# Sixteen gate/up steps placed beside the exponentials of an S4 + SwiGLU forward and backward kernel, with a re-laid prologue

## The chip, the cores and the metric

The kernel runs on one core of one Trainium2 chip. The metric is device time in microseconds for one launch; the figure of a kernel is the median of its runs. A profiled execution shows, for each engine (PE = TensorE, with its weight loads apart as PEld; DVE = VectorE; ACT = ScalarE; POOL = GpSimd; SP = SyncE, which here only issues transfers), what ran when and what it waited for.

## The reference

With x of 2048 tokens by D = 576 channels, N = 128 states, F = 4608 hidden units:

```python
xn = layernorm(x)                                  # no weights, eps 1e-5
dt = exp(log_dt)[:, None]
P  = exp((dt * A)[:, :, None] * arange(L))         # D x N x L, complex
K  = einsum("dn,dnl,dn->dl", C, P, dt * B).real    # the kernel of the convolution
s  = irfft(rfft(pad(xn)) * rfft(pad(K)))[:L] + xn * Dskip
gate, up = xn @ w1, xn @ w3
g  = silu((silu(gate) * up) @ w2)
out = x + s * g
```

The kernel returns `out` and, for a given `grad_out`, the gradients of x, of the seven S4 parameter matrices and vectors (real and imaginary parts apart), of Dskip, and of w1, w3, w2.

## The kernel before, in words

One program, in stages whose instructions a scheduler interleaves by priority. `pre(us)` and `at(us)` set the priority of what follows (`pre` for the prologue, in units of 600 for one us; `at` in units of 1000, behind all of `pre`). A `Chain` keeps the operations that go through it in program order on their engine, and `issue_after(x)` puts an instruction behind x in that order. So the order on an engine is fixed before the launch; on the chip each engine runs its list in order and waits by semaphores.

Prologue (`prologue`, L264). The 2048 tokens are 16 tiles of 128 rows; the odd tiles are held in reversed order of rows (`odd_A_u`, written by one transfer and read back). `ln_stats` (L169) and `ln_normalise` (L186) give `xn_bf` (tokens on partitions), and PE transposes, eight tiles at a time, give `xnT` (channels on partitions; its last 64 channels stand twice, the second copy made by an SP transfer). The S4 kernel is not evaluated state by state over 2048 points: l is split into two digits, and exp and the phases are made for short tables. For that, rho = dt · A_re is split into three bf16 pieces (`split3`, L374), stored (`PCS_dram`) and read back as `lhs_r`; a selector row matrix SELR (built from index rows) times `lhs_r` gives exponents in PSUM (`e_ps`, 128x1024 f32, two buffers), ACT takes the exponential (`early_exps`, L498; 54 of them, the product at L514), and the table goes to `E_dram` in 18 stores of 3072 columns. `early_spectra` (L519) multiplies folded sums of `xn_bf` (held in the `xt` tiles) by DFT matrices `cCS` (product at L533, eviction by DVE at L537) and stores the spectrum of the input, `UH_dram`.

Gate and up products (`ffn_hidden`, L859). 9 blocks of 512 hidden units by 8 pairs of token tiles are 72 steps. A step multiplies 2 tiles by 512 columns of w1 and of w3: 16 products 128x128x512 (L901) and 4 tail products for the last 64 channels (L909, two at a time on the two halves of the array). pg and pu, two PSUM buffers each, take them. ACT writes silu(gate) into s_t (L913), copies up into u_t (L918), and copies the gate of the first tile into g_t (L917); DVE copies the gate of the second (L915) and multiplies h_t = s_t · u_t (L920). H goes out on SP's queue, G and U on POOL's, for the backward pass.

Interleaved with it, by due times in its argument: `ssm_forward` (L469), which is `ssm_kernel` (L542) with 36 chunks of 16 channels, and then `ssm_conv` (L788). A chunk loads its part of `E_dram` (SP), makes phases by 12 products 128x256 (`et_ps`, L589), takes sines on ACT (`cs_k`, L590, six of 512 columns), multiplies on DVE (`q_k`, `p_k`, `t_k`, `v_k`), and sums over states by 64 small products (`kps`, L626). The convolution comes in two halves of the channels; each makes the spectra of the kernel, multiplies them with `UH_dram` on DVE (complex products, `cm_t` and `V`, L777 to L786), and transforms back (L761). Its small loads (Dskip, the reversed `grad_out`, the DFT matrices turned into `cT` over `CS_dram`) are issued on SP at the opening of `ssm_forward`. PSUM has eight banks of 512 f32 columns: beside the gates, `s_ps` (three) and `s_ps1` (one).

After both come `ffn_output` (L927, the product with w2 and the output) and `backward` (L1344).

Of the kernel before, what the change touches and what calls it, by code (L numbers as in the profile page):

```python
# [10 lines left out]
ACT = mybir.ActivationFunctionType  # L11
# [6 lines left out]
P = 128  # L18
# [58 lines left out]
class K:  # L77

# [47 lines left out]
    def setup_consts(self):  # L126
# [3 lines left out]
        self.pre(2)  # L130
# [4 lines left out]
        self.eps_col = const.tile([P, 1], FP32, name="eps_col")  # L135
        nc.vector.memset(self.eps_col[:], 1e-5)
# [6 lines left out]
        self.irow = const.tile([P, 512], FP32, name="irow")  # L143

    def pre(self, us):
        self.tc.cur_priority = int(us * 600)
# [9 lines left out]
    def ln_load(self, sb):  # L156
        nc, cfg = self.nc, self.cfg
        xf = self.aps["A_u"].flatten_outer_dims()
        self.xs, self.xts = [], []
        for b in range(cfg.LT // 4):  # L160
            xt = sb.tile([P, 4, cfg.D], BF16, name=f"xt{b}")
            rows = xf[4 * b * P:4 * (b + 1) * P, :].rearrange("(i two p) d -> two p i d", two=2, p=P)
            nc.sync.dma_start(out=xt[:, 0:4:2, :], in_=rows[0])
            self.xs += [xt[:, i, :] for i in range(4)]
            self.xts.append(xt)
        for b, xt in enumerate(self.xts):
            nc.sync.dma_start(out=xt[:, 1:4:2, :], in_=self.odd["A_u"][2 * b:2 * b + 2].rearrange("i p d -> p i d"))

    def ln_stats(self, sb, small):  # L169
        nc, cfg = self.nc, self.cfg  # L170
        D, LT = cfg.D, cfg.LT
        half = D // 2
        self.mv = sb.tile([P, LT, 2], FP32, name="mv")
        for i in range(LT):
            stats = small.tile([P, 2, 6], FP32, name="stats")
            self.V.bn_stats(stats[:, 0, :], self.xs[i][:, 0:half])
            self.V.bn_stats(stats[:, 1, :], self.xs[i][:, half:D])
            if i > 0:
                self.V.bn_aggr(self.mv[:, i - 1, :], last[:])
            last = stats  # L180
        self.V.bn_aggr(self.mv[:, LT - 1, :], last[:])
# [4 lines left out]
    def ln_normalise(self, sb, ps):  # L186
        nc, cfg = self.nc, self.cfg
        D, LT, DT = cfg.D, cfg.LT, cfg.DT
        nfull = D // P
        rem = D - nfull * P  # L190
        negmr = sb.tile([P, LT], FP32, name="negmr")
        self.V.scalar_tensor_tensor(out=negmr[:], in0=self.mv[:, :, 0], scalar=-1.0, in1=self.rstd[:], op0=ALU.mult,
                                       op1=ALU.mult)
        TB = 8
        for tb in range(0, LT, TB):
            for i in range(tb, tb + TB):
                self.V.tensor_scalar(out=self.xn_bf[:, i, :], in0=self.xs[i], scalar1=self.rstd[:, i:i + 1],
                                        scalar2=negmr[:, i:i + 1], op0=ALU.mult, op1=ALU.add)
            if tb > 0:
                self.dft_rows()  # L200
            tsl = slice(tb * P, (tb + TB) * P)
            for c, (do, dsz) in enumerate(cfg.dch):
                pt = ps.tile([P, TB * P], BF16, name="ln_pt")
                for j in range(TB):
                    nc.tensor.transpose(pt[:dsz, j * P:(j + 1) * P], self.xn_bf[:, tb + j, do:do + dsz],
                                        self.ident_bf[:])
                self.V.tensor_copy(out=self.xnT[:dsz, c, tsl], in_=pt[:dsz, :])
            nc.sync.dma_start(out=self.xnT[rem:P, nfull, tsl], in_=self.xnT[0:rem, nfull, tsl])
        for b in range(LT // 4):
# [54 lines left out]
    def prologue(self, matp, selp, xp):  # L264
# [6 lines left out]
        self.rstd = self.persist.tile([P, LT], FP32, name="rstd")  # L271
        self.xnT = xp.tile([P, DT, L], BF16, name="xnT")
        self.PCS_dram = self.dram.tile([3, 3, D, N], BF16, name="PCS_dram")
        mul = lambda e, o, a, b: e.tensor_tensor(out=o[:], in0=a[:], in1=b, op=ALU.mult)
        with pool(name="par_tmp", bufs=1) as tmp, pool(name="sel_tmp", bufs=1) as st, pool(name="ln_sb", bufs=1) as lsb, \
                pool(name="ln_small", bufs=4) as small, pool(name="dftgen", bufs=1) as dg, \
# [1529 lines left out]
```

## Time and profile before

| | us |
|---|---|
| median of 3 runs (lowest to highest) | 1875.47 (1872.55 to 1878.48) |
| the profiled execution, own time | 1874.95 |
| its span | 1873.2 |
| PE busy, share of the span | 1689.1, 90% |
| DVE busy | 1370.1, 73% |
| ACT busy | 910.0, 49% |
| POOL busy | 352.1, 19% |
| first product of the exponentials | starts at 35.59 |
| last exponential | starts at 126.15 |
| first gate product | 126.98 |
| first sine of a kernel chunk (cs_k) | 152.26 |
| last v_k of the chunks | starts at 428.11 |
| first product of the output stage | 601.45 |

How to read it: the whole-span shares average over stages with different limits, so the table gives the edges of the stages too; they come from the timeline (start, duration, engine, line, operation, output <- inputs, and in brackets the idle time before and what ended it). A group's row in the view by line has, behind the count, the busy time, the mean of one in ns, and the idle time of its engine just before it with what ended it. The view by stretch gives, for each, the engines' busy time, the granted clock of PE, the busy share of the 16 DMA engines, and GB/s.

### The profile page before, as it was taken

How to read it: one execution, taken by the hardware profiler on the slowest of the kernel's cores; microseconds unless marked ns; L12 is line 12 of the kernel's file. 1: busy time of each engine (PE TensorE's matmuls, PEld its weight loads, DVE VectorE, ACT ScalarE, POOL GpSimd, SP SyncE). 2: the span in 40 equal slices, each digit the busy share in tenths (PEclk: the TensorE clock that was granted, in tenths of full speed). 3: DMA queues.
4: the chain of work that ended last, by engine and by line, in shares of the span. 5: the costliest groups of instructions: out<-in, count | busy, mean ns of one | idle time of the engine just before them, and what ended most of it. 6: DMA issues, size and time to landing. Idle time of an engine off the chain costs nothing. (4 is left out here: it accounts for less than half of the span.)

```text
span 1873.2 us, 38325 instructions
## 1 busy us (share of the span) xinstructions
PE 1689.1 (90%) x15461; PEld 1231.2 (66%) x15516; DVE 1370.1 (73%) x2081; ACT 910.0 (49%) x1632; POOL 352.1 (19%) x567
## 2 busy tenths in 40 slices
PE   2999999999897999799999999999998968979997
PEld 0335555555353777578878887888777756868786
DVE  5538666768988555588694989759998954867675
ACT  3768888887563111465765756565444300001001
POOL 4021222222223111011111111111110242031032
PEclk9999999999998999899999999999999998989999
DMA  6579988887777997658666575579999899988993
GB/s 172 175 242 328 328 304 305 308 291 267 239 242 225 218 205 179 218 157 232 183 198 190 180 211 173 167 210 284 258 233 232 179 221 245 209 195 204 220 210 72
DMA packets 627231, 417.27 MB, mean 223 GB/s; under 512 B 424429, under 2 KB 567853, under 8 KB 622445
## 3 DMA queue, kind: packets, MB, share of 16 engines
q1 hardware_dynamic: 569820, 281.98, 58.3%
q0 software_dynamic: 30672, 106.50, 16.8%
q10 hardware_dynamic: 26560, 26.35, 4.7%
q8 instruction: 121, 1.98, 0.4%
q14 instruction: 58, 0.47, 0.1%
HBM read 135.74 MB, written 190.89 MB: 174 GB/s over the span
## 5 line engine op out<-in xcount | busy, mean ns | idle before, releaser
L1657 PEld LDWEIGHTS <-acts 128*128 128x128 bf16 x2304 | 228.4, 100 | 100.7 <-DMA acts<-GG_dram 19.8
L1610 PEld LDWEIGHTS <-xn_bf 128*128 128x128 bf16 x2304 | 225.6, 98 | 37.0 <-issue 10.1
L1229 DVE TENSOR_TENSOR pr_q<-et_ps,pz 128x1024 f32<-128x1024 f32 x144 | 176.0, 1222 | 48.9 <-PE et_ps L1224 41.8
L1657 PE MATMUL px<-wT,acts 128*128 128x288 bf16 x1408 | 182.5, 289 | 17.3 <-DMA wT<-in_B_w_dram 17.3
L901 PEld LDWEIGHTS <-xnT 128*128 128x128 bf16 x1152 | 107.4, 98 | 115.5 <-issue 25.3
L1232 DVE TENSOR_REDUCE S_all<-pr_q 128x32 f32<-128x1024 f32 x144 | 175.3, 1217 | 3.4
L1552 PE MATMUL ph<-w2T,goT 128*128 128x256 bf16 x1440 | 173.0, 275 | 1.6 <-ACT gh L1555 1.4
L901 PE MATMUL pg<-wmB_w,xnT 128*128 128x512 bf16 x526 | 147.9, 382 | 16.4 <-DVE g_t L915 9.5
L901 PE MATMUL pu<-wmB_w,xnT 128*128 128x512 bf16 x571 | 155.4, 379 | 0.4
L1590 PE MATMUL pgw<-go_o,h_n 128*128 128x288 bf16 x1152 | 150.4, 287 | 4.1 <-DVE h_n L1530 2.8
L1552 PEld LDWEIGHTS <-goT 128*128 128x128 bf16 x1440 | 140.4, 99 | 19.7 <-issue 2.8
L1610 PE MATMUL pgw<-gu_n,xn_bf 128*128 128x256 bf16 x1152 | 135.6, 276 | 7.0 <-ACT gw L1594 6.8
L1657 PE MATMUL px<-wA,acts 128*128 128x288 bf16 x896 | 123.4, 298 | 19.6 <-DMA acts<-GG_dram 19.1
L1590 PEld LDWEIGHTS <-h_n 128*128 128x128 bf16 x1152 | 112.6, 98 | 32.5 <-DVE h_n L1530 3.3
L1610 PE MATMUL pgw<-gg_n,xn_bf 128*128 128x256 bf16 x1152 | 130.2, 273 | 1.6 <-ACT gw L1612 1.6
L913 ACT ACTIVATE s_t<-pg 128x512 bf16<-128x512 f32 x144 | 87.8, 610 | 89.4 <-PE pu L909 44.7
L1685 ACT ACTIVATE go<-gx 128x576 bf16<-128x576 f32 x16 | 10.9, 683 | 220.7 <-DVE gx L1668 220.7
L1555 ACT CAST gh<-ph 128x512 bf16<-128x512 f32 x144 | 82.0, 600 | 71.6 <-PE ph L1552 54.0
L590 ACT ACTIVATE cs_k<-et_ps 128x512 bf16<-128x512 int16 x216 | 112.1, 643 | 1.7 <-PE et_ps L589 1.3
L1612 ACT CAST gw<-pgw 128x256 bf16<-128x256 f32 x144 | 53.9, 375 | 99.3 <-PE pgw L1610 96.7
L924 POOL DMA_DIRECT2D G_dram<-g_t x72 | 52.3, 727 | 232.3 <-DVE g_t L915 223.9
L918 ACT CAST u_t<-pu 128x512 bf16<-128x512 f32 x144 | 86.9, 604 | 12.0 <-PE pu L901 12.0
(302 smaller groups left out, 3232.2 us busy)
## 6 DMA issues: line engine op xcount, KB each, us to landing
U_dram<-u_t POOLq DMA_DIRECT2D x72, 256.0 KB, 4.3
G_dram<-g_t POOLq DMA_DIRECT2D x72, 256.0 KB, 4.0
H_dram<-h_t SPq DMA_DIRECT2D x72, 256.0 KB, 4.7
Q_dram<-q_k SPq DMA_DIRECT2D x36, 512.0 KB, 4.2
h_n<-U_dram POOLq DMA_DIRECT2D x18, 1024.0 KB, 8.7
gg_n<-G_dram POOLq DMA_DIRECT2D x18, 1024.0 KB, 5.9
GU_dram<-gu_n SPq DMA_DIRECT2D x36, 512.0 KB, 3.6
GG_dram<-gg_n SPq DMA_DIRECT2D x36, 512.0 KB, 8.3
```

The source lines that it names most:

```text
L590: nc.scalar.activation(out=CS[:, :, o:o + 256], in_=pt[:].bitcast(I16)[:, :, 0::2], func=ACT.Sin, scale=6.283184 / 2 ** 16)
L901: ins = nc.tensor.matmul(pt[:], lhsT=xnT[:, c, ts], rhs=wm[w][:, c, :], start=(q == 0 and c == 0), stop=(q == 1 and c == nfull - 1))
L913: nc.scalar.activation(out=s_t[:, :, q, :], in_=pgv, func=ACT.Silu)
L918: nc.scalar.copy(out=u_t[:, :, q, :], in_=pu[:].rearrange("p (g f) -> p g f", g=ng))
L1229: nc.vector.tensor_tensor(out=pr[:].rearrange("p r k e -> p r (k e)"), in0=T[h][:].rearrange("p k z d a -> p (k z d a)")[:, None].to_broad ...
L1232: nc.vector.tensor_reduce(out=self.S_all[:, :, d0:d0 + 4], in_=pr[:].rearrange("p r k (d a) -> p (r k) d a", d=4), op=ALU.add, axis=AX.X)
L1552: self.pe_last = nc.tensor.matmul(ph[j][:, k, :].rearrange("p (a f) -> p a f", f=P), lhsT=lw, rhs=rh, start=(n == 0), stop=(n == nfull))
L1555: self.sc(lambda: nc.scalar.copy(out=gh[:, j], in_=ph[j][:]))
L1590: self.pe_last = nc.tensor.matmul(pgw[pi_][:, 0:pw], lhsT=hn[:, tt, fl * P:(fl + 1) * P], rhs=go_o[:, tt, po:po + pw], start=(tt == 0), st ...
L1610: self.pe_last = nc.tensor.matmul(pw_[:, 0:FG], lhsT=self.xn_bf[:, tt, c * P:(c + 1) * P], rhs=nat[:, tt, :], start=(tt == 0), stop=(tt == ...
L1612: self.sc(lambda: nc.scalar.copy(out=gw[:, c], in_=pw_[:, 0:FG]))
L1657: self.pe_last = nc.tensor.matmul(px[pi_][:, 0:pw], lhsT=act[:, ai, fi, :], rhs=w[:, po:po + pw], start=(n == 0), stop=(n == len(steps) - 1))
```

## The change

- The first 16 of the 72 gate/up steps (two blocks) are placed in the prologue, each tied by `issue_after` to one of the exponentials. ACT uses Tanh there in place of Silu, since it stands beside Exp: silu(g) = g · (0.5 tanh(g/2) + 0.5). POOL multiplies g · u, DVE does the rest. g_t is copied by ACT in the first four of these steps, by DVE in the others. G is stored on SP's queue, U on POOL's. In the first block a step takes two tiles of the same parity, and G and U are stored in two transfers each.
- PSUM: the gates' four banks are open in the prologue; `e_ps` has one buffer (two banks) instead of two, and one pool `t_ps` of two banks serves the transposes and the spectra, whose evictions are cut into 64 of 288 columns.
- Layer norm: even tiles first, then odd; 1/sqrt by an integer shift and three Newton steps on DVE instead of a square root on ACT; transposes four tiles at a time; the second copy of the last 64 channels is made by PE; the folded sums are made by POOL.
- Index rows are made in bf16 by POOL, in place of i32 rows and ACT casts; log_dt is loaded as rows and turned by PE. The queues: even x tiles, ten parameter loads, six stores of pieces and three `lhs_r` loads on SP; log_dt and A_re on ACT's; odd tiles and the first weights on POOL's.
- Each exponential is stored by itself (54 stores instead of 18). The convolution's small loads stand on SP behind chunk 8's load of its table.
- The other 56 steps follow a plan by hand: 38 beside the 36 chunks, 18 beside the convolution, each tied to a chunk's or a transform's last product. In the chunk stage ACT copies the gate of the first tile in two steps of three, DVE the others; in the convolution ACT copies all.

```diff
+    EARLY = 16
...
-        self.tc.cur_priority = int(us * 600)
+        self.tc.cur_priority = int(us * 1000)
...
-        sd = sb.tile([P, LT], FP32, name="sd")
-        self.S.activation(out=sd[:], in_=self.mv[:, :, 1], func=ACT.Sqrt, bias=self.eps_col[:], scale=1.0)
-        self.V.reciprocal(out=self.rstd[:], in_=sd[:])
...
+        V.tensor_scalar(out=a[:].bitcast(I32), in0=v[:].bitcast(I32), scalar1=1, scalar2=None, op0=ALU.logical_shift_right)
+        V.tensor_scalar(out=y.bitcast(I32), in0=a[:].bitcast(I32), scalar1=-1.0, scalar2=float(0x5f3759df), op0=ALU.mult,
+                        op1=ALU.add)
+        for _ in range(3):
+            V.scalar_tensor_tensor(out=a[:], in0=y, scalar=-0.5, in1=y, op0=ALU.mult, op1=ALU.mult)
+            V.tensor_tensor(out=a[:], in0=a[:], in1=v[:], op=ALU.mult)
+            V.scalar_tensor_tensor(out=y, in0=a[:], scalar=1.5, in1=y, op0=ALU.add, op1=ALU.mult)
...
+        for t0 in range(0, len(tiles), 4):
+            four = tiles[t0:t0 + 4]
+            xT = self.xnT.rearrange("p c (t q) -> p c t q", q=P)[:, :, four[0]:four[-1] + 1:2]
+            lead = self.exps[leads[t0 // 4]]
...
+                    for j, i in enumerate(four):
+                        with self.tc.issue_after(lead.ins) if c + j == 0 else nullcontext():
+                            nc.tensor.transpose(pv[:, j * P:(j + 1) * P], self.xn_bf[:, i, c * P:(c + 1) * P], self.ident_bf[:])
+                else:
+                    pv = pt[:]
...
-                self.V.tensor_tensor(out=self.xts[b][:, 2 * k:2 * k + 2, :], in0=lo, in1=hi, op=op)
+                self.G.tensor_tensor(out=self.xts[b][:, 2 * k:2 * k + 2, :], in0=lo, in1=hi, op=op)
...
-                pool(name="ex_l", bufs=1) as lp, pool(name="ex_e", bufs=3) as ep, pool(name="ex_u", bufs=2) as up, \
-                pool(name="ex_ps", bufs=2, space=PS) as eps, ExitStack() as early:
-            lps = early.enter_context(pool(name="ln_ps", bufs=2, space=PS, side="right"))
...
+                pool(name="ex_ps", bufs=1, space=PS) as eps, pool(name="t_ps", bufs=2, space=PS) as tps:
...
+            pd = tps.tile([P, 512], FP32, name="t_ps")
+            nc.tensor.transpose(pd[:].bitcast(BF16)[:, 0:DT], lr[:], self.ident_bf[0:DT, 0:DT])
+            self.S.activation(out=self.dt_col[:], in_=pd[:].bitcast(BF16)[:, 0:DT], func=ACT.Exp)
...
-            self.dma_engines, self._dma_i = [nc.sync, self.S], 0
+            self.dma_engines, self._dma_i = [nc.sync], 0
             self.split3(tmp, rho, 2)
-            self.S.copy(out=self.irow[:], in_=irow[:])
-            self.dft_angles()
-            for k, eng in enumerate((nc.sync, self.S, nc.sync)):
-                ld = eng.dma_start(out=LR_[k * 16:(k + 1) * 16],
-                                   in_=self.PCS_dram[2, k].rearrange("(k p) n -> p k n", p=16))
+            for k in range(3):
+                nc.sync.dma_start(out=LR_[k * 16:(k + 1) * 16], in_=self.PCS_dram[2, k].rearrange("(k p) n -> p k n", p=16))
+            self.dft_phases()
+            self.build_reader(SELR)
+            self.pre(6)
+            self.load_rates(tmp)
+            self.A_im = self.load_dmat(tmp, aps["A_A_im"], "A_im", fill=0.0)
             self.pre(8)
-            self.build_reader(SELR, st)
-            self.pre(10)
-            self.dft_phases()
-            self.pre(12)
+            self.dft_sines()
+            self.pre(9)
+            last = self.ln_stats(even[1:], small, last)
+            self.ln_root(even, small, last)
+            self.early_exps(SELR, LR_, ep, eps, 0, 4)
+            self.pre(18)
+            self.ln_normalise(even, tps, (2, 4))
+            self.pre(24)
+            last = self.ln_stats(odd, small)
+            self.ln_root(odd, small, last)
+            self.ln_normalise(odd, tps, (7, 10))
             self.dft_signs()
-            self.build_selectors(st, selp)
-            self.dma_engines = [nc.sync]
-            with self.tc.issue_after(ld.ins):
-                self.A_im = self.load_dmat(tmp, aps["A_A_im"], "A_im", fill=0.0)
+            self.dft_rows()
+            self.pre(30)
...
+            self.early_exps(SELR, LR_, ep, eps, 4, 12)
+            self.pre(75)
...
+            self.early_exps(SELR, LR_, ep, eps, 12, 18)
+            self.pre(42)
+            self.ln_fold()
+            self.build_selectors(st, selp)
+            self.pre(60)
...
+            self.early_spectra(up, tps, 50, 1.15)
+            self.exps_last = self.S.prev
+            for n in range(self.EARLY + 1):
+                next(gate)
...
+        self.sel_dl = dl = st.tile([P, QW + 2 * PW], BF16, name="sel_dl")
+        self.sel_val = val = st.tile([P, QW + 2 * PW], BF16, name="sel_val")
...
+        sync.prev = after
...
+        sync.dma_start(out=self.odd["grad_out"][:], in_=self.turned(self.aps["grad_out"].flatten_outer_dims()))
+        self.CS_dram = self.dram.tile([2, 2, P, cfg.LS], BF16, name="CS_dram")
+        sync.dma_start(out=self.CS_dram[:].rearrange("m i p k -> p m i k"), in_=self.cCS[:])
+        self.cT = self.matp.tile([P, 2, cfg.KT, 2 * P], BF16, name="cT")
+        for m in range(2):
+            for i in range(2):
+                sync.dma_start_transpose(out=self.cT[:, m, :, i * P:(i + 1) * P], in_=self.CS_dram[m, i])
...
+            self.exps, self.e_stores = [], []
+            self.E_dram = self.dram.tile([NCH // 2, P, 2 * TW], BF16, name="E_dram")
         for c2 in range(2 * p0, 2 * p1, 2):
...
+                e = len(self.exps)
+                self.pre(17.5 + 1.2 * e if e < 7 else 26 + 4 * (e - 7) if e < 12 else 46 + 1.9 * (e - 12))
+                E = ep.tile([P, 1024], BF16, name="E_k")
...
+                self.exps.append(self.e_last)
+                self.S.activation(out=E[:], in_=pe[:], func=ACT.Exp)
+                self.e_stores.append(nc.sync.dma_start(out=self.E_dram[c2 // 2, :, o:o + 1024], in_=E[:]))
...
+                        self.pre(T + TU * (((h * NB + m) * KT + kt) * 2 + ri))
+                        pt = ps.tile([P, 512], FP32, name="t_ps")
...
+                if ch == 8:
+                    self.conv_loads(el)
...
+                ins = nc.tensor.matmul(pt[:, k], lhsT=lhs, rhs=SEL[:, k, o:o + 256], start=True, stop=True)
+            with self.tc.issue_after(self.exps_last.ins):
+                nc.scalar.activation(out=CS[:, :, o:o + 256], in_=pt[:].bitcast(I16)[:, :, 0::2], func=ACT.Sin,
+                                     scale=6.283184 / 2 ** 16)
+        self.marks.append(ins)
...
-            self.at(T0 + TC * b)
+            self.at(T0 + TC * 4.5 * b)
...
-            self.at(T0 + TC * (NB + m))
+            self.at(T0 + TC * (18, 23, 35, 52)[m])
...
+    def gate_time(self, n):
+        if n < 4:
+            return -74 + 5 * n
+        if n < self.EARLY:
+            return -54 + 6.5 * (n - 4)
+        i = n - self.EARLY
+        return 19.2 + 7 * i if i < 38 else 285 + 8.2 * (i - 38)
+
+    def gate_mark(self, n):
+        i = n - self.EARLY
+        if i < 38:
+            return 36 * i // 38 - 1
+        h, k = divmod(i - 38, 9)
+        return 36 + 8 * h + (-1 if k == 0 else (1, 3, 4, 4, 5, 5, 6, 6)[k - 1])
+
...
+            ld = Chain(self.tc, nc.sync if fb else nc.gpsimd)
+            ld.prev = self.x_last if fb == 0 else self.e_stores[10] if fb == 1 else None
...
+                    mark = self.gate_mark(step)
+                    while due is not None and (due <= T or len(self.marks) <= mark):
+                        due = next(self.ssm, None)
+                pair = [4 * (n % 4) + n // 4 + 2 * q for q in range(NT)] if fb == 0 else [NT * n, NT * n + 1]
+                early = step < self.EARLY
...
+                if early:
+                    th = self.dftgen.tile([P, ng, NT, self.FG], BF16, name="th", tag=("dft_fr", "dft_q")[step % 2])
...
+                                    lead = None
+                                    if c + q == 0 and w == "B_w1":
+                                        if early:
+                                            lead = self.exps[6 + 3 * step // 2 if step < 4 else 12 + 7 * (step - 4) // 2]
+                                        else:
+                                            lead = self.marks[mark] if mark >= 0 else None
+                                    with self.tc.issue_after(lead.ins) if lead else nullcontext():
+                                        ins = nc.tensor.matmul(pt[:], lhsT=xnT[:, c, ts], rhs=wm[w][:, c, :],
+                                                               start=(q == 0 and c == 0), stop=(q == 1 and c == nfull - 1))
...
-                    nc.scalar.activation(out=s_t[:, :, q, :], in_=pgv, func=ACT.Silu)
-                    if q % 2 == 1:
+                    if early:
+                        nc.scalar.activation(out=th[:, :, q, :], in_=pgv, func=ACT.Tanh, scale=0.5)
+                    else:
+                        with self.tc.issue_after(self.exps_last.ins):
+                            nc.scalar.activation(out=s_t[:, :, q, :], in_=pgv, func=ACT.Silu)
+                    if step < 4 or step >= self.EARLY + 38 or (not early and q == 0 and step % 3):
+                        nc.scalar.copy(out=g_t[:, :, q, :], in_=pgv)
+                    else:
                         nc.vector.tensor_copy(out=g_t[:, :, q, :], in_=pgv)
-                    else:
-                        nc.scalar.copy(out=g_t[:, :, q, :], in_=pgv)
                     nc.scalar.copy(out=u_t[:, :, q, :], in_=pu[:].rearrange("p (g f) -> p g f", g=ng))
                 self.tail = chain
-                nc.vector.tensor_tensor(out=h_t[:].rearrange("p t (g f) -> p g t f", g=ng), in0=s_t[:], in1=u_t[:],
-                                        op=ALU.mult)
-                nc.sync.dma_start(out=self.H_dram[i0:i0 + NT, :, f0:f0 + FB].rearrange("t p f -> p t f"), in_=h_t[:])
+                hv = h_t[:].rearrange("p t (g f) -> p g t f", g=ng)
+                if early:
+                    nc.gpsimd.tensor_tensor(out=s_t[:], in0=g_t[:], in1=u_t[:], op=ALU.mult)
+                    self.at(T + 7)
+                    nc.vector.tensor_scalar(out=hv, in0=th[:], scalar1=0.5, scalar2=0.5, op0=ALU.mult, op1=ALU.add)
+                    nc.vector.tensor_tensor(out=hv, in0=hv, in1=s_t[:], op=ALU.mult)
+                else:
+                    nc.vector.tensor_tensor(out=hv, in0=s_t[:], in1=u_t[:], op=ALU.mult)
+                tsl = slice(pair[0], pair[-1] + 1, pair[1] - pair[0])
+                nc.sync.dma_start(out=self.H_dram[tsl, :, f0:f0 + FB].rearrange("t p f -> p t f"), in_=h_t[:])
                 for (dst, src) in ((self.G_dram, g_t), (self.U_dram, u_t)):
-                    nc.gpsimd.dma_start(out=dst[fb * ng:(fb + 1) * ng, :, i0:i0 + NT, :].rearrange("g p t f -> p g (t f)"),
-                                        in_=src[:].rearrange("p g t f -> p g (t f)"))
+                    if early and src is g_t:
+                        self.at(T + 3)
+                    eng = nc.sync if early and src is g_t else nc.gpsimd
+                    if fb:
+                        eng.dma_start(out=dst[fb * ng:(fb + 1) * ng, :, tsl, :].rearrange("g p t f -> p g (t f)"),
+                                            in_=src[:].rearrange("p g t f -> p g (t f)"))
+                    else:
+                        for g in range(ng):
+                            eng.dma_start(out=dst[g, :, tsl, :], in_=src[:, g])
...
+            gate = k.ffn_hidden(wp, gup, fps)
+            k.prologue(matp, selp, xp, gate)
...
-                k.ffn_hidden(wp, gup, fps, 0, 12, k.ssm_forward(0, 8, 8))
+            k.ssm = k.ssm_forward(21, 7.3, 1)
+            for _ in gate:
+                pass
```

More of the change, by code (lines that the diff above doesn't have):

```diff
@@ L166, in ln_load, with ln_load_odd @@
+        self.xs = [xt[:, i, :] for xt in self.xts for i in range(4)]
+    def ln_load_odd(self):
         for b, xt in enumerate(self.xts):
[L167 to L174, printed above, removed]
+            self.x_last = self.nc.gpsimd.dma_start(out=xt[:, 1:4:2, :],
+                                                   in_=self.odd["A_u"][2 * b:2 * b + 2].rearrange("i p d -> p i d"))
@@ L175, in ln_stats @@
+    def ln_stats(self, tiles, small, last=None):
+        half = self.cfg.D // 2
+        for i in tiles:
             stats = small.tile([P, 2, 6], FP32, name="stats")
             self.V.bn_stats(stats[:, 0, :], self.xs[i][:, 0:half])
[L177 to L181, printed above, removed]
-        sd = sb.tile([P, LT], FP32, name="sd")
@@ new lines, in ln_stats, with ln_root @@
+            self.V.bn_stats(stats[:, 1, :], self.xs[i][:, half:])
+            if last is not None:
+                self.V.bn_aggr(self.mv[:, last[0], :], last[1][:])
+            last = i, stats
+        return last
+    def ln_root(self, tiles, small, last):
+        self.V.bn_aggr(self.mv[:, last[0], :], last[1][:])
+        sl = slice(tiles[0], tiles[-1] + 1, 2)
+        self.root(small, self.rstd[:, sl], self.mv[:, sl, 1], len(tiles))
+        self.V.scalar_tensor_tensor(out=self.negmr[:, sl], in0=self.mv[:, sl, 0], scalar=-1.0, in1=self.rstd[:, sl],
+                                    op0=ALU.mult, op1=ALU.mult)
```

285 lines of the change are left out of this document (129 added, 156 removed).

## The prediction

> **What bounds the kernel now.** First view: busy time of each engine by stretch of the span; the columns are stretch, length, busy us (and instructions) of PE, PEld, DVE, ACT, POOL, granted clock, DMA share, GB/s.
>
> ```profile
> 0.00:36.00 36.00, 0.41 (x2) 0.17 (x3) 24.22 (x86) 6.18 (x7) 16.94 (x26) 1.00 0.67 181
> 36.00:127.00 91.00, 85.17 (x271) 26.42 (x270) 39.33 (x73) 65.45 (x69) 12.83 (x17) 1.00 0.58 197
> 127.00:152.00 25.00, 24.64 (x136) 12.23 (x138) 17.20 (x30) 13.22 (x24) 4.38 (x6) 1.00 0.76 255
> 152.00:428.00 276.00, 266.76 (x3513) 150.09 (x3547) 197.82 (x275) 241.03 (x478) 66.80 (x92) 1.00 0.89 310
> 428.00:601.00 173.00, 153.06 (x915) 79.10 (x930) 158.72 (x217) 96.55 (x202) 41.12 (x56) 0.96 0.73 239
> 601.00:1873.00 1272.00, 1159.10 (x10633) 963.16 (x10631) 932.76 (x1404) 487.53 (x855) 210.00 (x371) 0.97 0.81 204
> ```
>
> Five stages precede 601. PE is empty for 36 us. From 36 to 127 it looks full with only 271 instructions. From 152 to 428 (kernel chunks beside gate steps) PE is the bound. From 428 to 601 (convolution beside the last gate steps) VectorE is, 158.7 of 173. Next, the timeline where the first stage opens and where it closes:
>
> ```profile
> 35.59 1.86 PE L514 MATMUL e_ps<-SELR,lhs_r 48*128 48x512 bf16 x4 [35.59 <-DVE stats L72]
> 36.63 1.94 ACT L72 ACTIVATE E_k<-e_ps 128x1024 bf16<-128x1024 f32 x2 [17.23 <-PE e_ps L514]
> ...
> 126.15 1.02 ACT L72 ACTIVATE E_k<-e_ps 128x1024 bf16<-128x1024 f32 x1 [1.50 <-PE e_ps L514]
> 126.98 0.63 PE L901 MATMUL pg<-wmB_w,xnT 128*128 128x512 bf16 x1
> ```
>
> So the 54 exponentials run from 36.6 to 127.2 and the first gate product starts behind the last of them. The first line's releaser (stats) is only the last event seen; lhs_r was issued at 23.3 to 27.4 and lands at about 35, and that is the true wait. Then the groups by line from 36 to 127, the PE groups from 104 to 126.9, and a gate product's from 152 to 428:
>
> ```profile
> L514 PE MATMUL e_ps<-SELR,lhs_r 48*128 48x512 bf16 x108 | 54.2, 613 | 39.0 <-DVE stats L72 35.6 <-ACT E_k L72 2.3 <-ACT WT L72 1.0
> L72 ACT ACTIVATE E_k<-e_ps 128x1024 bf16<-128x1024 f32 x54 | 54.1, 1025 | 40.8 <-PE e_ps L514 40.5 <-ACT E_k L72 0.2
> ```
> ```profile
> L514 PE MATMUL e_ps<-SELR,lhs_r 48*128 48x512 bf16 x30 | 15.0, 614 | 0.7 <-ACT E_k L72 0.7
> L533 PE MATMUL u_ps<-xt,cCS 128*128 128x288 bf16 x30 | 8.8, 440 | 0.0
> ```
> ```profile
> L901 PE MATMUL pu<-wmB_w,xnT 128*128 128x512 bf16 x350 | 96.5, 379 | 0.1
> ```
>
> ACT idles 40 us for the e_ps product, and that product takes 613 ns, where the gate product of the last view, of the same 512 columns, takes 379. PE is at half rate throughout this stage, though the clock column, which shows what the throttle granted, says 1.00. Last, the rows of the convolution stage:
>
> ```profile
> L783 DVE TENSOR_TENSOR cm_t<-u,kz 128x2304 bf16<-128x2304 bf16 x20 | 26.8, 1344 | 0.0
> L915 DVE CAST g_t<-pg 128x512 bf16<-128x512 f32 x24 | 16.2, 677 | 1.2 <-ACT s_t L913 1.2
> L920 DVE TENSOR_TENSOR h_t<-s_t,u_t 128x1024 bf16<-128x1024 bf16 x24 | 16.1, 671 | 0.3 <-ACT u_t L918 0.3
> ```
>
> VectorE spends 32 us there on gate steps; its own work has no idle before it.
>
> **The change part by part.** Unit prices, as pitches from start to start: a gate step on PE is 16 full products at 0.2155 us plus 0.53 for the tails, 3.98; a chunk on PE is 12 × 0.109 (et_ps) + 64 × 0.0186 (kps) + gaps, 2.7. Check: 44.7 steps and 36 chunks make 275 against the 276.5 us measured (152.3, first cs_k, to 428.8, last v_k). On VectorE a step is 1.2 us (g_t 0.6 on average, h_t 0.6).
>
> A. Start of the exponentials, 35.6 → 27 (20 to 32). log_dt comes by rows and a PE transpose, so dt_col leaves the chain near 5 instead of 11.3, and the pieces of rho are ready by about 10. Against that, the built order puts four xt loads and ten rate loads ahead of the six PCS stores, on SP alone. At 0.6 to 0.9 us an issue (the eight rate loads took 12.96 to 20.16 before) they reach SP at 12 to 15.5 (20.2 before), the lhs_r loads at about 18 (23.4), and they land 8 after their issue, as before (27.4 to 35).
>
> B. End of the prologue, first cs_k, 152.3 → 165. The two versions differ in kind here: before, four gate steps were done by 152; now sixteen are. From 27: seven exponentials at 2.2 us (the product now waits for the activation, since e_ps has one buffer: 1.0 cold product + 1.03 + hand-off) are 15. Steps 0 to 3, with five exponentials and the odd tiles' transposes, are 24. Twelve steps with 3.5 exponentials each follow. Their PE work at full rate is 3.98 + 3.5 × 0.43 + 10.7 spectra products at 0.128 = 6.9 us; ACT's is 3.5 × 1.03 + four evictions at a pitch of 0.48 = 5.5. I take 8.0, for the waits of a single e_ps: 3.5 rounds of product, hand-off and activation at 1.8 are 6.3, which PE can't always fill. 12 × 8.0 = 96, the WT turn 3: 165, so **+12.7** (bounds 140 to 195). Tanh has no row; an eviction of the same tile costs 593 to 612 ns (Silu, copies), and I take that, down to nothing if another engine is last. Its new POOL product has no row either: POOL's 128x640 products take 1.26 to 1.53 us, so 2.0 to 2.5 for 128x1024, sixteen times, and with the folds moved there POOL is under 90 us of 138, off the path. The two VectorE operations of a step (0.7 each) and u_e copies cut into 64 halves leave VectorE at about 110 of 138. The root on VectorE adds 12 tiny operations, twice, under 0.2 us each, beside exponentials; it takes away a Sqrt.
>
> C. Kernel chunks, 276.5 → 250, **−26.3**. 37 steps × 3.98 + 36 × 2.7 = 244.5; plus 2 of edges, plus 4 where the grad_out turn, the CS store and the four cT transposes now stand on SP between chunk 8's and chunk 9's E loads. q_k waits for those loads, and v_k, kps behind it. Bounds 0 and 12. ACT then has 36 × 3.4 + 37 × 2.4 = 211 of 250 and covers the g_t copies still put there.
>
> D. Convolution, 172 → 156, **−16**. VectorE's own work is 128.5 (two halves of 64.3), plus 25 × 1.2 and 13 idle: 172 now. Eighteen steps are left and their g_t go to ACT: 128.5 + 18 × 0.6 + 17 idle. Idle 12 to 20 gives 151 to 160.
>
> E. From the first output product (601.4) the built order of instructions is the same on all engines: 0, with ±3 left for its transfers (DMA is 81% busy there).
>
> Sum: 12.7 − 26.3 − 16 = −29.6 on the profiled execution's 1874.95 (span 1873.2): 1845.4. That execution lies 0.03% below the median of the three runs, 1875.47, so no correction: **1845**.
>
> **The rivals.**
>
> Full packing. If PE never waits and is at full rate, the prologue ends at 27 + 113 = 140 (16 × 3.98 of gates, 108 × 0.2155 of e_ps, 128 × 0.128 of spectra, 10 of transposes): −12.3 − 26.3 − 16 = −54.6, **1820**. For it: gate products reached 379 ns within 1.5 us of starting at 127. Against it: one e_ps buffer, and e_ps and u_ps rows that stayed cold from 104 to 126.9 while PE was busy 23.8 of 22.9 us. Chance 0.20. [...]
>
> Cold prologue, the slower side. PE stays at half rate beside exponentials, as in all of 36 to 127, because 48-row products and waits interrupt the gate products. A step is then 7.9 + 3.5 × 0.85 + 10.7 × 0.245 = 13.5 us; 12 make 162, the prologue ends near 244, +92 − 42 = +50: **1924**. It decides once a step takes over 8.0 + 29.6/12 = 10.5 us, which is about half of the time cold. For it: rate held only at 73 to 79% busy or more elsewhere, and a 3 us gap at 510 cost it (granted clock 0.76 to 0.90 after). Against it: of a step's 6.9 us, 3.98 are products of the form that warmed at once. Chance 0.14.
>
> Transfers become the bound. DMA is 0.89 busy at 310 GB/s in the chunk stage; the same bytes in 26 us less need about 320 or more (337 was seen), and eight of the early steps store G and U in rows of 512 B instead of 1024, G on SP between the E stores. Chunks then stay at 265 to 276: 1860 to 1871, **1866**, and up to 1885 if E loads wait for the last E stores. Chance 0.12.
>
> The gain in chunks is given back in the convolution: VectorE has 128.5 of its own, and if its idle time grows from 13 to 33 us, for ACT now has every g_t there, D is nothing: **1861**. Chance 0.08. That the gates would not be moved at all is excluded: the built order shows sixteen steps before the first cs_k.
>
> **How the numbers follow.** The forecast, 1830 to 1860, has 0.46. Faster by over 0.3% (about what a measurement of this kernel can tell from no change) is the forecast, full packing, the convolution case and four tenths of the transfer case: 0.79. Within 0.3% (1870 to 1881): 0.06, from transfers and a half-cold prologue. Slower: 0.15. The range goes from 1816 (full packing with idle 12 in D) to 1877 (transfers, or two fifths of the prologue cold).
>
> **What would show it.** First exponential at 27; first cs_k at 165, with e_ps products at 613 (cold) or 379 (warm) ns and the gate products the same; ACT's idle before E_k named e_ps; last v_k at 415; first output product at 572; everything behind it of equal length. It is wrong if the products from 50 to 150 stay above 600 ns, if the chunks do not reach 7 us each, or if the last stage shifts with the layout of the early stores.

## The result, and the profile after

The changed kernel took 1967.88 us in the median of four runs (1961.28 to 1985.62), the kernel before 1876.97 beside it. The ratio is 1.0503, 95% interval 1.0429 to 1.0577. The forecast, 1845 us and a range up to 1877, had the wrong sign.

The view by stretch of the changed kernel, cut at its first cs_k, last v_k, first output product and first ph product (the first product of the backward part):

```profile
0.00:229.30 229.30, 153.12 (x682) 54.60 (x695) 138.65 (x286) 110.99 (x149) 111.90 (x102) 0.90 0.59 191
229.30:492.30 263.00, 244.62 (x3365) 140.64 (x3401) 195.18 (x279) 219.42 (x434) 55.89 (x77) 0.96 0.88 299
492.30:668.30 176.00, 132.16 (x799) 70.31 (x809) 141.38 (x188) 87.41 (x190) 38.15 (x52) 0.88 0.71 207
668.30:844.60 176.30, 157.09 (x1260) 120.68 (x1260) 90.13 (x143) 25.32 (x54) 23.98 (x46) 0.97 0.77 189
844.60:1961.90 1117.30, 1005.01 (x9372) 845.60 (x9370) 841.08 (x1258) 461.26 (x800) 179.17 (x317) 0.96 0.81 201
```

The reader is to see that PE has less work from 229 on, as planned, and that no stretch is full any more: in the prologue PE is busy 153 of 229 us and POOL 112, where POOL had 34 before. The same five lengths for all kernels (us; profiled executions):

| kernel | prologue | chunks | convolution | output | backward | span |
|---|---|---|---|---|---|---|
| before | 152.3 | 276.5 | 172.7 | 167.0 | 1104.7 | 1873.2 |
| after | 229.3 | 263.0 | 176.0 | 176.3 | 1117.3 | 1961.9 |
| e1 folds on DVE | 212.8 | 260.6 | 175.3 | 175.9 | 1114.9 | 1939.5 |
| e2 POOL cleared | 189.4 | 260.5 | 171.9 | 176.3 | 1131.9 | 1930.0 |
| e3 four early | 202.6 | 292.9 | 163.7 | 174.0 | 1119.4 | 1952.6 |
| e4 loads early | 229.3 | 248.3 | 174.1 | 175.6 | 1115.4 | 1942.7 |
| e5 halves | 244.3 | 262.4 | 174.8 | 177.7 | 1121.5 | 1980.7 |
| e6 halves, POOL cleared | 196.9 | 262.4 | 175.1 | 178.0 | 1121.5 | 1933.9 |
| e7 e6, loads early, S on POOL | 198.3 | 248.5 | 172.7 | 182.5 | 1126.7 | 1928.7 |
| e8 before again | 152.7 | 276.6 | 172.8 | 167.5 | 1104.6 | 1874.2 |
| e9 before, one e_ps | 173.5 | 283.2 | 172.0 | 171.1 | 1119.6 | 1919.4 |
| e10 two e_ps, POOL cleared, loads early | 187.2 | 248.4 | 175.9 | 176.4 | 1115.2 | 1903.1 |
| e11 e10, H load held | 184.0 | 247.3 | 165.4 | 176.7 | 1117.7 | 1891.1 |
| e12 before, 54 stores | 150.8 | 278.6 | 172.1 | 168.5 | 1114.1 | 1884.1 |
| e13 e11, H loads in order | 185.3 | 247.3 | 164.5 | 167.6 | 1131.0 | 1895.7 |
| e14 e13 with four early | 161.6 | 276.2 | 162.1 | 190.9 | 1115.7 | 1906.5 |

Against before, the change is +77.0, −13.5, +3.3, +9.3 and +12.6: 88.7 us of span. The lengths come from one profiled execution each; e7, e13 and e14 have four timed runs, the other experiments the profiled one alone. The kernel before, timed beside them, took 1902.32 us (e1 to e4, one run), 1881.30 (e5 to e8), 1876.33 (e9 to e12, one run) and 1881.38 (e13, e14), so the lengths of stages are compared, not the totals.

### The profile page after: what moved, and what is told of

Its sections match the earlier page's. It is cut to its first block, busy times and chain, and to the rows that moved or that the text cites. A ratio compares the mean times of both kernels' runs of the same rounds, so it can differ in the third digit from the quotient of the medians.

```text
span 1961.9 us, 38537 instructions
## 1 busy us (share of the span) xinstructions
PE 1692.0 (86%) x15472; PEld 1231.8 (63%) x15533; DVE 1406.4 (72%) x2153; ACT 904.4 (46%) x1625; POOL 409.1 (21%) x594
## 5 line engine op out<-in xcount | busy, mean ns | idle before, releaser
L1328 DVE TENSOR_TENSOR pr_q<-et_ps,pz 128x1024 f32<-128x1024 f32 x144 | 176.0, 1222 | 53.7 <-PE et_ps L1323 46.2
L982 PE MATMUL pg<-wmB_w,xnT 128*128 128x512 bf16 x524 | 155.2, 402 | 23.3 <-ACT g_t L1000 16.3
L1020 POOL DMA_DIRECT2D G_dram<-g_t x56 | 40.6, 725 | 289.3 <-DVE g_t L1002 163.9
L1694 POOL DMA_DIRECT2D out_dram<-gw x36 | 20.0, 555 | 372.0 <-ACT gw L1693 319.1
```

What stands on the lines that cost most here:

```text
L982: ins = nc.tensor.matmul(pt[:], lhsT=xnT[:, c, ts], rhs=wm[w][:, c, :], start=(q == 0 and c == 0), stop=(q == 1 and c == nfull - 1))
L1020: eng.dma_start(out=dst[fb * ng:(fb + 1) * ng, :, tsl, :].rearrange("g p t f -> p g (t f)"), in_=src[:].rearrange("p g t f -> p g (t f)"))
L1328: nc.vector.tensor_tensor(out=pr[:].rearrange("p r k e -> p r (k e)"), in0=T[h][:].rearrange("p k z d a -> p (k z d a)")[:, None].to_broad ...
```

## The experiments

**Theory 1**, formed on the trace of after: operations of POOL stop VectorE's, and PE stands behind them. Its lines in the timeline of the changed kernel (start, duration):

```profile
60.89 2.11 POOL L1007 TENSOR_TENSOR s_t<-g_t,u_t 128x1024 bf16<-128x1024 bf16 x1 [1.08 <-ACT u_t L1003]
...
61.06 1.97 DVE L72 SCALAR_TENSOR_TENSOR rt_a<-rstd 128x8 f32<-128x8 f32 x1
...
64.03 13.09 DVE L72 TENSOR_SCALAR xn_bf<-xt,rstd,negmr 128x576 bf16<-128x576 bf16 x8
...
64.97 11.99 POOL L72 TENSOR_TENSOR xt<-xn_bf 128x1152 bf16<-128x1152 bf16 x5 [0.55 <-DVE xn_bf L72]
```

```profile
86.87 7.00 POOL L72 TENSOR_TENSOR xt<-xn_bf 128x1152 bf16<-128x1152 bf16 x3
...
88.06 0.14 DVE L72 TENSOR_SCALAR rp<-pcol 128x1 f32<-128x1 f32 x1
...
88.30 5.59 DVE L72 TENSOR_TENSOR rp<-rp,rc 128x1 f32<-128x1 f32 x1
...
94.11 0.16 DVE L72 TENSOR_TENSOR rs<-rs,rc 128x1 f32<-128x1 f32 x1
```

A root step of eight columns, usually 0.17 us, lasts 1.97 and ends with the POOL product at 63.0. A product of one column with two inputs lasts 5.59 us and ends with the last of three folds at 93.9, without getting in between them; the same form takes 0.16 when POOL is idle. An operation with a single input, at 88.06 beside the same folds, takes its 0.14. So this is no sharing of bandwidth: the operation waits until the other engine's has ended. The xn_bf operations, with one tensor as input, show the same: 13.09 us for eight of them, five of which last 2.46 us each, one beside each of five folds, where the others last 0.42; before, all eight took 2.81:

```profile
54.69 2.81 DVE L72 TENSOR_SCALAR xn_bf<-xt,rstd,negmr 128x576 bf16<-128x576 bf16 x8
```

Waits of the changed kernel from 30 to 229 us (total, times, longest) show how this reaches PE: its spectra products wait for VectorE's evictions u_e. They also show a second cost of POOL, VectorE's wait for the product g · u itself:

```profile
DVE h_t L1010 <- POOL s_t L1007: 23.5, 14, 2.6
PE t_ps L570 <- DVE u_e L574: 20.9, 18, 4.4
```

**Theory 2**: the single e_ps buffer, whose product and activation exclude each other (in the changed kernel the first activation runs from 33.59 to 34.61 us, and the next two products start at 34.67), and PE at half rate in between. By half rate is meant what the kernel before shows: four spectra products beside the exponentials span 1.14 us (at 106.32), and 0.65 after the first gate products (at 136.06).

e1 and e2 put POOL's work back:

```diff
-                self.G.tensor_tensor(out=self.xts[b][:, 2 * k:2 * k + 2, :], in0=lo, in1=hi, op=op)
+                self.V.tensor_tensor(out=self.xts[b][:, 2 * k:2 * k + 2, :], in0=lo, in1=hi, op=op)
# e2, besides:
-                    nc.gpsimd.tensor_tensor(out=s_t[:], in0=g_t[:], in1=u_t[:], op=ALU.mult)
+                    nc.vector.tensor_tensor(out=s_t[:], in0=g_t[:], in1=u_t[:], op=ALU.mult)
-                self.G.tensor_scalar(out=self.SEL[:, k, sl], ...
+                self.V.tensor_scalar(out=self.SEL[:, k, sl], ...
```

> Only the eight folded sums go back from POOL to VectorE. Theory 1 (while POOL reads SBUF, VectorE's two-input and fast one-input operations stand still, and PE behind them): the eight xn_bf operations take 0.42 us each again (13.1 us together after the change, 61 to 77 us), the 5.6 us stall of a 128x1 operation at 88 us goes, and the first cs_k comes 15 to 25 us earlier than 229.3, total about 1945. Theory 2 (the single e_ps buffer and PE at half rate between gate products set the length): durations may change but the first cs_k stays within 5 us of 229, total 1960 to 1970.

> Folded sums, the sixteen products g*u and the selector operations all go from POOL to VectorE; POOL keeps the W products and its transfers. Theory 1: no VectorE operation between 60 and 230 us takes more than its usual duration, the 20.9 us that h_t waited for s_t and the 20.9 us that t_ps waited for u_e shrink to under 8 each, first cs_k at 180 to 195, total 1915 to 1930. Theory 2: first cs_k at 220 or later, total above 1950.

Measured: prologues of 212.8 and 189.4 us, 16.5 and 39.9 shorter, as theory 1 had it; the totals are 1941.24 and 1931.96, the second 2 us above its range. In e1 the xn_bf operations are quick again:

```profile
60.49 2.81 DVE L72 TENSOR_SCALAR xn_bf<-xt,rstd,negmr 128x576 bf16<-128x576 bf16 x8
```

In e2 PE hardly waits for the evictions any more (30 to 189 us):

```profile
PE t_ps L570 <- DVE u_e L574: 3.2, 11, 0.8
```

e2 gives VectorE 28 operations more than it had, and the prologue is shorter for it. That POOL's work cost these 39.9 us is shown (e4, which keeps it, has a prologue of 229.3 again). How they divide is not: e2 takes away the standing still of VectorE and also h_t's 23.5 us of waiting for POOL's product. For the folds alone, e1's 16.5 us go with five xn_bf operations at 2 us more than usual and the 5.59.

e3 leaves four early steps: `EARLY = 4`, with 46 steps planned beside the chunks and 22 beside the convolution.

> Only four gate steps are left in the prologue, as many as ran before the first cs_k in the kernel before; 46 then stand beside the chunks and 22 beside the convolution. The rest of the re-laid prologue stays. Theory 1: the folds on POOL still stall VectorE, so the first cs_k comes at 160 to 175, later than the 152.3 of before in spite of an earlier first exponential; chunk stage about 275, total 1890 to 1920. Theory 2: without twelve steps beside the exponentials the prologue is as long as before or shorter (140 to 152), total 1860 to 1885.

Both theories missed: 202.6 us, longer than either gave. The e_ps products average 538 ns from 33 to 185 us, where the kernel before had 613 for them beside its exponentials and the changed kernel a median of 376; by these numbers about two thirds of them ran at half rate (an estimate). The same four steps without POOL's work, with two buffers and the small loads in the prologue (e14, below) end at 161.6; which of these gave the 41 us was not separated.

e5, e6 and e7 were to tell the single buffer. They hold one e_ps tile and empty it by halves:

```diff
-                pe = ps.tile([P, 1024], FP32, name="e_ps")
+                pe = self.pe                     # one tile, kept
-                self.S.activation(out=E[:], in_=pe[:], func=ACT.Exp)
+                for k in range(2):
+                    self.S.activation(out=E[:, 512 * k:512 * k + 512], in_=pe[:, 512 * k:512 * k + 512], func=ACT.Exp)
```

> e_ps stays at two banks, but is held as two halves of 512 columns, each with its own exponential of 512 columns, so that a product can fill one half while ACT empties the other. POOL keeps its work. Early4 showed the re-laid prologue ending at 202.6 with only four gate steps in it, 50 us later than before; theory 2 (the exclusive turn of product and activation on a single e_ps buffer, with PE cold between) then gives 10 to 30 us here: first cs_k at 200 to 220. Theory 1 (POOL's locks on VectorE alone) leaves it at 225 to 235; 54 more activations add up to 10 us of ACT.

> The halves of e5 and POOL cleared as in e2 (first cs_k 189.4). If the two causes are separate, their gains add: first cs_k at 160 to 178. If the same wait was counted twice, it stays at 183 to 190.

By themselves they say nothing on theory 2, since the next pair of products still started behind the second activation (0.1 us). They measure what 54 more activations cost: 15.0 us (244.3, after 229.3) and 7.5 (196.9, e2 189.4).

e9 asks it in the kernel before (`bufs=2` to `bufs=1` for `ex_ps`), e10 with two real buffers in the repaired kernel:

```diff
-                pool(name="ex_ps", bufs=1, space=PS) as eps
+                pool(name="ex_ps", bufs=2, space=PS) as eps
-                pe = ps.tile([P, 1024], FP32, name="e_ps")   # one product and activation of 1024
+                    pe = ps.tile([P, 512], FP32, name="e_ps")   # each of the two of 512
```

> The kernel before with one e_ps buffer instead of two and nothing else. If the exclusive turn of product and activation is what the re-laid prologue pays, an exponential costs about 2.2 us plus the spectra products between (0.5 to 1.0 us at half rate) instead of the 1.66 us of before: first cs_k at 185 to 205 instead of 152.3, and the time 1905 to 1930. If the half rate of PE alone sets it, first cs_k stays below 165. From the first ph product to the end: 1105 if the timing of the early stages has no part in that stretch's loss, 1112 or more if it has.

> The changed kernel with two separate e_ps buffers of 512 columns (in e5 to e7 both halves were still released together, the next pair of products starting 0.1 us behind the second activation), POOL cleared as in e2, the small loads in the prologue as in e4. By the single-buffer theory an exponential costs 1.2 us (two activations of 0.6) instead of 1.83, a gate step 7.0 to 7.8 instead of 9.3, and the first cs_k comes at 160 to 175 instead of 189.4. If PE's own work and its switches between small groups are the bound by now (it was busy 22.4 of 25 us in e2), 182 to 190.

One buffer costs the kernel before 20.8 us of prologue (173.5 against e8's 152.7), between the two cases I gave. In the repaired kernel, e10 is 2.2 us ahead of e2 (187.2 against 189.4), but that is the net of two things: e10 has 54 more activations. Against e6 and e7, which have them too, the second buffer gives 9.7 and 11.1 us. So theory 2 is right for about 10 us, which the activations take back to the greater part; it is not the 14 to 29 us that I gave it. With POOL's work in place no run had two buffers. What is left is PE, busy 96% of the time from 33 to 165 us of e10:

```profile
33.00:165.00 132.00, 126.80 (x599) 45.19 (x598) 99.92 (x242) 92.61 (x172) 26.83 (x37) 0.99 0.73 244
```

Busy is not peak, though: the same products count 147.5 us of PE up to the first cs_k in e10 and 140.1 in e2, where the prediction summed 113 for full rate. A single e_ps product between others:

```profile
125.58 0.39 PE L552 MATMUL e_ps<-sel_val,lhs_r 48*128 48x512 bf16 x1
125.90 0.42 PE L572 MATMUL t_ps<-xt,cCS 128*128 128x288 bf16 x2
```

From the start of the e_ps product to the start of the next group it is 0.32 us, where the prediction had 0.2155.

e4 moves the small loads:

```diff
-                if ch == 8:
-                    self.conv_loads(el)
+            self.conv_loads(self.e_stores[20])       # in the prologue
```

> The reversed grad_out, the DFT matrices' store and the four cT transposes are issued on SP in the prologue, behind the 21st exponential's store, instead of behind chunk 8's load of its table. If these transfers made the hole at 305 to 330 us (PE 16.7 of 25 us busy, q_k and cs_k waiting), the chunk stage goes from 263 to about 253 us, total about 1953; the rival, that the hole belongs to the chunk's own chain, leaves 263.

Chunks of 248.3 instead of 263.0. In the changed kernel's timeline one sees why:

```profile
301.92 7.68 SPq L72 DMA_TRANSPOSE cT<-CS_dram  x4
...
310.28 0.46 SPq L607 DMA_DIRECT2D E_l<-E_dram  x1
...
314.18 0.69 DVE L636 TENSOR_TENSOR p_k<-cs_k,E_l 128x1024 bf16<-128x1024 bf16 x1 [0.73 <-DMA E_l<-E_dram]
```

The transposed loads hold SP's queue for 7.7 us, the next table load stands behind them, and in the hole PE is busy for 16.7 of 25 us (305 to 330) at a granted clock of 0.66.

The convolution, in the changed kernel:

```profile
599.84 19.34 SPq L1588 DMA_TRANSPOSE hcA<-H_dram  x1
...
600.21 2.26 POOL L1053 DMA_DIRECT2D w2a<-in_B_w_dram  x3 [4.21 <-PE et_ps L771]
...
609.47 16.60 ACTq L893 DMA_DIRECT2D S_dram<-s_t  x2
...
624.85 0.45 DVE L891 TENSOR_TENSOR s_t<-ev,et_ps 128x288 bf16<-128x288 f32 x1 [15.62 <-DMA S_dram<-s_t]
...
626.75 1.87 PE L982 MATMUL pg<-wmB_w,xnT 128*128 128x512 bf16 x4 [15.32 <-ACT g_t L1000]
```

All three engines stand still for 15 us. Before, the transposed load of H came 18 us after the first of the four w2 loads (576 KB each; issued from 541.06 on) and took 5.1 us:

```profile
559.53 5.11 SPq L1489 DMA_TRANSPOSE hcA<-H_dram  x1
```

With fewer steps left, its last input is ready sooner, and it now meets them. e7 moved the S stores to POOL's queue (`nc.scalar` to `nc.gpsimd`), e11 held the H load instead:

```diff
+                with self.tc.issue_after(self.h_68.ins) if i == 0 else nullcontext():
                     self.hc_loads.append(self.nat_transpose(hc[:], self.H_dram[i]))
```

> e6, with the convolution's small loads in the prologue (e4: chunk stage 247.6 instead of 263) and the S stores on POOL's queue instead of ACT's. If the 16 us hole of the convolution at 610 to 626 comes from ACT's in-order wait at the S store's issue, the convolution goes from 176 to 155 to 162 us; if the transposes of H and the w2 loads hold the DMA engines anyway, to 170 to 176. Total 1860 to 1900, from about equal to the kernel before to 1% slower.

> e10, with the first transposed load of H ordered behind the H store of step 68, so that it no longer meets the four loads of w2 (597 KB each; in the changed kernel it was issued at 599.84, they at 600.2 to 605.4, and its issue took 19.3 us against 5.1 before). If that meeting makes the hole of the convolution, the stretch from the last v_k to the first output product goes from 173 to 176 us to 155 to 165. If not, it stays above 170.

e7 left the stretch at 172.7 us (total 1932.41, ratio 1.0257, 1.0182 to 1.0332): the queue of the S store was not the cause. e11 made it 165.4, 10.5 us shorter than e10: the meeting of the loads was.

e13 orders the first three H loads A, B, C; e14 is the same with four early steps.

> e11, with the transposed loads of H in the order A, B, C (in e11 C went ahead of B, B's issue took 14.8 us, and the output stage took 176.7 us from its first product to the first ph instead of 167.5). Expected: prologue 184, chunks 247, convolution 166, output 167 to 170, total 1880 to 1890: within 1% of before, and not faster.

> The same repairs with four early gate steps instead of sixteen. If the moved steps cost in the prologue what they save later (about 4.4 us each beside the exponentials against 2.5 to 4 us each later), the prologue ends at 130 to 140, the chunks take 276, the convolution 160 to 170, and the total is 1870 to 1885, equal to e13 or up to 15 us better. If the prologue without them is no shorter than 155 because PE turns cold, e14 is slower than e13 by 5 us or more.

e13: the output stage is back at 167.6, and the first ph product starts at 764.7, 4.9 us ahead of e8's. Still its total is 1900.84 us, above the 1880 to 1890 expected, ratio 1.0126 (1.0063 to 1.0189), since the backward part took 1131.0 in the profiled run. e14: 1903.21, ratio 1.0117 (1.0061 to 1.0173). Up to the first output product e13 needs 597.1 and e14 599.9: twelve moved steps cost 23.7 us of prologue and 2.4 of convolution and give 28.9 of chunks, net 2.8. e14's prologue of 161.6 missed the 130 to 140 expected and is 9 us longer than that of before with as many early steps, so the re-laid prologue is no gain by itself. From 100 to 125 us e14 has no gate step, and PE's granted clock is 0.53:

```profile
100.00:125.00 25.00, 21.70 (x70) 7.64 (x70) 9.41 (x21) 13.01 (x25) 5.45 (x8) 0.53 0.75 254
```

e14's output stage, 190.9 us, is 23.3 longer than e13's, which is not the early steps' own cost. Its second load of H meets the other five w2 loads (they are issued from 591.65 on), takes 20.2 us to issue, and PE waits 22.5 us for it:

```profile
589.52 20.24 SPq L1591 DMA_TRANSPOSE hcB<-H_dram  x1
...
626.47 6.87 PE L1077 MATMUL po<-w2a,hcB 128*128 128x288 bf16 x32 [22.52 <-DMA hcB<-H_dram]
```

Their backward parts differ by 15 us as well, the other way. So the near equal totals of e13 and e14 are no measure of what the twelve steps are worth; the 2.8 us up to the first output product are a better one.

**The backward part.** e8 and e12 asked why 1104.7 became 1117.3 under the same order of instructions.

> The kernel before, unchanged, on the chip of these runs. From its first ph product to the end it took 1104.7 us in the first profile, the changed kernel and e1, e3, e4 1115 to 1119, e2 1132. If the change lengthens the backward part, this run gives 1105 to 1108; if it is the chip or the run, 1112 or more.

> The kernel before with each exponential stored by itself (54 stores instead of 18), as the changed kernel does. The prologue and the chunks should not move by more than 3 us. From the first ph product to the end, 1104.6 us in both runs of before and 1115 to 1132 in all with the change: if the number and size of the stores on SP's queue shift that stretch, 1112 or more, else 1105.

It is not the chip alone: on e8's chip before took 1104.6 again, and e5 to e7, on the same one, 1121.5 to 1126.7. But e12, with prologue and chunks within 2.1 us of e8's, took 1114.1, and e9 1119.6. In e13 most of the loss falls in one stretch in which the DMA engines are full (in the kernel before, from 1315 to 1440 us, their busy share reads 1.08 at 251 GB/s): by the starts of the same VectorE operations, about 21 of its 26 us. In e12 that stretch loses under 1 us; most of its 9.5 fall before and behind it. The waits of e13 (1310 to 1445 us) and of e8 (1315 to 1440), each with total, times, longest:

```profile
PE et_ps L1326 <- DMA gz<-gK_dram: 15.5, 3, 6.4
```

```profile
PE et_ps L1224 <- DMA gz<-gK_dram: 6.9, 3, 4.4
```

The gz loads stand on SP behind transposed loads; two of these took 17.7 us to issue in e13, where no row in e8's stretch has more than 9.5. These waits differ by 8.6 us, less than half of the loss. Other runs of before beside these, whose traces are not kept, ranged from 1871 to 1902 us, so one execution each can't tell a part of this from chance. What makes the backward part longer in every variant stays open.

## Why the prediction was wrong

- A, start of the exponentials: 27 forecast, 32.55 measured, half a us outside its bounds of 20 to 32. The PCS stores came at 15.2 as worked out; lhs_r waited for their landing until 26.4, where I had put its issue at 18.
- B, the step that failed: "with the folds moved there POOL is under 90 us of 138, off the path". POOL's busy time (measured: 112 of 229 us) was weighed as if it cost VectorE nothing. Clearing it (e2) gives back 39.9 of the 64.3 us by which 229.3 exceeds 165. The other 24.4, read off e2 by the first Tanh of a step: the fifth step starts at 72.6, where 66 was forecast (6.6, of which the later start of the exponentials is 5.0); from there to the sixteenth step, at 175.3, it is 102.7 with the WT turn between, where eleven steps of 8.0 and 3 for the turn make 91 (11.7); and from there to the first cs_k 14.1 instead of one step (6.1). So the step at 8.0 was too cheap as well: in e10, which has a second buffer, it is 8.8 with the turn between, where the forecast makes 8.3, and PE is busy 96% of the time, with 0.32 us for a lone e_ps product instead of 0.2155.
- The rivals: PE mostly cold was priced at 244 us (its terms as written, 27 + 15 + 24 + 162 + 3, make 231), near the measured 229, but that is luck, it was not the mechanism: e_ps products had a median of 376 ns. The granted clock was low in the stretches from 50 to 125 us (0.73 to 0.84), where VectorE stood still, and 0.86 to 1.00 there in e2 and 0.93 to 1.00 in e10.
- C, −26.3 forecast, −13.5 measured. The mechanism was right, the term mis-sized: the small loads with the transposes between chunk 8 and 9 cost 14.7 (e4), where the sum had 4 and bounds 0 to 12. Without them it is −28.2, where the sum without its 4 has −30.3.
- D, −16 forecast, +3.3 measured. VectorE's work fell as worked out (158.7 to 141.4); idle rose to 35, as in the rival of the convolution, though for 10.5 of it not for ACT's copies: that was the transposed load (e10 to e11). Even without it, in e13, VectorE is idle for 23 us, where the forecast had 17. Its waits for ACT's kraw, ev and u_t are 14.7 us there and were 7.8 before, so a part of the rival may hold; no run tested it.
- E, 0 ± 3: the order behind the first output product is the same, but two H loads ahead of it had changed places, 9 us (e11 to e13). The backward 12.6 is unexplained.
- The gain to be had was small in any case. Of the twelve steps between e14 and e13, eight left the chunks, where 28.9 us came back for 31.8 of products; four left the convolution, where VectorE is busy for 141.5 us instead of 143.7 and nothing came back (162.1 to 164.5); and the prologue took 23.7 for all twelve.

## What to carry to other kernels

Before work goes to POOL, list what VectorE does at that time: in this kernel VectorE's two-input operations and its one-input bf16 operations xn_bf and h_t, where they came up during one of POOL's two-input operations, ended only with it, however short they were (a root step 1.97 us for 0.17, xn_bf 2.46 for 0.42, h_t 2.13 for 0.42). When steps leave a stage, look for the transfers whose last input now comes sooner, above all transposed loads, and for what they meet (here one took 19.3 us to issue instead of 5.1). And price a stage that is filled with small products of several shapes by their start-to-start times in such a mixture (0.32 us for a lone e_ps product here, not 0.2155).

## What was not expected of the hardware

A VectorE product of one column lasted 5.59 us beside three of POOL's folds, of 2.4 us each, and did not get in between them. A transposed load of H took 19.3 us to issue beside four w2 loads and 5.1 without them. In e14, from 100 to 125 us, e_ps and spectra products lasted 600 and 413 ns at a granted clock of 0.53 with PE busy 21.7 of 25 us; in e10, from 125 to 150, they lasted 384 and 288 at 1.00, busy 23.8 of 25.
